# Moving the lower half of x to TensorE, converting two weight slices instead of four ahead of group 1, and taking scores ahead of y, in the ramp of a retention-plus-MLP kernel

## The chip, the cores and the metric

The kernel runs on one core of a Trainium2 chip. The metric is device time in microseconds (us) of one execution. Medians are quoted with the lowest and highest run.

## The reference

```python
def retnet(q, k, v):                 # each (4, 8, 768, 64): batch, head, position, dim
    for t in range(768):
        state = gamma[head] * state + outer(k[t], v[t])
        y[t]  = q[t] @ state / sqrt(64)

x = y.transpose(0, 2, 1, 3).reshape(3072, 512)
h = x @ w_in                         # w_in (512, 2048)
g = h * sigmoid(h)
out = g @ w_out                      # w_out (2048, 512)
```

The result must be close to float32, and the weights arrive as 64-bit floats, which the kernel puts together from their 32-bit words.

## The kernel before

The attention is computed in chunks of 128 positions. A *unit* is one chunk of one of 4 batches; the 24 units run through a pipeline of three stages, and a *visit* `m` does one stage of each of three units. Each float32 operand of the MLP becomes three fp32r parts (high, low, and a mixed term), so a *product* of a group `c` of 512 positions with a *slice* `f` of 128 columns of w_in is 12 matmuls: 8 into bank `ha`, 4 into `hb`. A slice costs eight VectorE instructions and three on ScalarE (`take_w`).

```python
def visit(m):
    first, mid, last = (0 <= m - i < len(units) for i in range(3))
    if first:
        stage_t(m)                       # transposes of k and q
    if last:
        scores, states_with, yp = stage_y(m - 2)
        scores()                         # y, first part
    if mid:
        sc, sums = score_tile(m - 1)
        stage_s(m - 1, sums)             # k^T v of both halves
    if last:
        states_with(0)                   # y, second part
    if mid:
        stage_a(m - 1, sc)               # scores
        ...
        finish_a(m - 1, sc, sums)        # VectorE: mask am, state
        scale_q(m - 1)                   # VectorE; at a new chunk GpSimd first scales gq
    ...
    if last:
        states_with(1)                   # y, third part
        finish_y(m - 2, yp)              # copy y, split it into x's three parts
```

The parts of y add into one pair of banks of PSUM, in which the kernel places TensorE's results. Between two parts stands a fence: GpSimd writes a one-element `token` when the last matmul of one part is done, and the next part waits for the token. GpSimd also makes the decay `gq` of the next chunk:

```python
def fence(done, then):
    i = nc.gpsimd.memset(token, 0.0).ins     # after done, ahead of then

def next_chunk():
    nc.gpsimd.tensor_tensor(out=gq, in0=gq, in1=step..., op=mult)
```

The order of TensorE's instructions is as written. On the other engines a list scheduler fixes an order of the instructions when the program is built. The trace of the kernel before fits that: ScalarE was idle for 3.27 us up to 33.66 us, where a step of a weight slice came, though y's last matmul had ended at 31.18 us; the copy of y ran at 35.58, behind two steps of that slice. The ramp:

```python
first = {6: (0, 0), 7: (0, 1), 8: (0, 2), 9: (0, 3)}
for m in range(10):
    if m in (0, 2, 4, 6):
        take_w()                         # four slices in the ramp
    visit(m)
    if m in first:
        product_in(*first[m])            # one product behind each of visits 6 to 9
...
pairs = [(1, f) for f in range(4)]       # then (1, f), each followed by visit 10 + f
```

## Time and profile before

| | before |
|---|---|
| median of the runs beside the change | 659.8 us (658.86 to 661.53) |
| profiled span | 658.1 us |
| TensorE busy | 619.1 us |
| TensorE idle | 39 us |

The prediction below shows where the idle time lies. In the views of the profile PE is TensorE (PEld its weight loads), DVE VectorE, ACT ScalarE and POOL GpSimd. A line gives start and length in us, engine, line of the kernel, operation, what it writes and reads, and in brackets the idle time before it and what ended it; "issue" means that the profile names nothing. Two more views are needed later. First, busy time by stretch. The columns are the stretch, its length, then busy us and count of PE, PEld, DVE, ACT and POOL, then the granted clock, the DMA share and GB/s:

```profile
20.00:45.00 25.00, 17.73 (x504) 15.71 (x501) 22.54 (x42) 12.76 (x25) 1.94 (x9) 0.80 0.87 197
45.00:80.00 35.00, 31.52 (x657) 25.87 (x659) 30.04 (x54) 21.35 (x37) 1.75 (x9) 1.00 0.73 182
80.00:140.00 60.00, 56.26 (x578) 46.10 (x569) 53.62 (x97) 37.20 (x66) 1.51 (x7) 0.97 0.64 186
```

VectorE (the third pair) is busy for 22.54 of 25 us in the first stretch. Second, GpSimd in order of time. It has next to nothing to do (14.5 us in all), so nothing in the page points to it:

```profile
36.69 1.04 POOL L280 TENSOR_TENSOR gq<-gq,step 128x512 f32<-128x512 f32 x1 [6.01 <-DVE qt L324]
37.67 0.09 POOL L307 MEMSET token<- 1x1 f32 x1
```

Already here the token runs right behind the decay multiplication, which had waited for VectorE (`qt`). TensorE was itself held until about 36 us, by a late copy of y, so it cost little.

### The profile page before, as it was taken

What the parts mean: (1) busy time and instruction counts of PE and PEld (TensorE: products, weight loads), DVE (VectorE), ACT (ScalarE), POOL (GpSimd) and SP (SyncE); (2) the same over time, 40 slices, a digit from 0 to 9 for tenths busy, and PEclk for the clock granted to TensorE, in tenths of its full rate; (3) what the DMA queues carried; (4) which work ended last, traced back from release to release, by engine and by line L of the source; (5) the groups of instructions that cost most, each with busy time, mean ns of one, the idle gap of its engine ahead of it and who ended that gap; (6) DMA issues with size and microseconds to landing.
All of it is one profiled execution on the core that took longest, in us unless ns stands there. A gap on an engine that the chain in (4) does not pass through costs nothing.

```text
span 658.1 us, 13540 instructions
## 1 busy us (share of the span) xinstructions
PE 619.1 (94%) x5440; PEld 509.5 (77%) x5440; DVE 429.4 (65%) x736; ACT 287.7 (44%) x522; POOL 14.5 (2%) x94
## 2 busy tenths in 40 slices
PE   4779989899999899999989999999999999999996
PEld 3667778788877777888768888888888888888885
DVE  3898899876968867667958856555463645554631
ACT  4556556655645344445437873222131412222311
POOL 3000000000000000000000000000000000000000
PEclk9879999999999899999999999999999999999999
DMA  9978685553477865757746744342342432433301
GB/s 202 215 163 209 169 213 167 167 185 128 172 260 171 215 179 162 225 176 218 242 135 202 205 162 151 97 161 96 97 159 97 136 121 96 160 90 103 128 0 65
DMA packets 123071, 103.65 MB, mean 157 GB/s; under 512 B 80000, under 2 KB 88192, under 8 KB 123008
## 3 DMA queue, kind: packets, MB, share of 16 engines
q1 hardware_dynamic: 119552, 96.49, 50.8%
q10 hardware_dynamic: 3456, 6.29, 2.6%
q8 instruction: 43, 0.70, 0.5%
q14 instruction: 20, 0.16, 0.1%
HBM read 66.06 MB, written 36.70 MB: 156 GB/s over the span
## 4 chain that ended last, share of the span: by engine, by line
PE 68%; DVE 17%; ACT 6%; DMA 5%; issue 3%; SPq 1%; ACTq 0%; DVEq 0%; POOLq 0%; POOL 0%
PE ha L489 15%; PE hb L489 8%; PE ob L620 7%; PE oa L618 7%; PE o L618 7%; PE o L620 7%; PE o L619 7%; PE oa L619 7%; DVE cs L200 2%; DVE cp L204 2%; DVE g L494 2%; DMA wf<-in_moe_w_in_dram 2%; PE y L391 2%; ACT g L495 1%; DMA wf<-in_moe_w_out_dram 1%
## 5 line engine op out<-in xcount | busy, mean ns | idle before, releaser
L489 PE MATMUL ha<-xt,wi 128*128 128x512 f32 x768 | 196.2, 397 | 6.4 <-DVE g L494 3.9
L489 PEld LDWEIGHTS ha<-xt,wi 128*128 128x128 f32 x768 | 142.8, 189 | 41.4 <-DVE g L494 7.3
L540 DVE TENSOR_TENSOR gs<-gr,gs 128x512 fp32r<-128x512 f32 x96 | 62.2, 686 | 90.3 <-ACT gs L538 90.3
L538 ACT ACTIVATE gs<-gr 128x512 fp32r<-128x512 f32 x96 | 53.5, 621 | 134.2 <-issue 131.8
L489 PE MATMUL hb<-xt,wi 128*128 128x512 f32 x384 | 103.4, 391 | 3.0 <-ACT g L493 2.8
L494 DVE TENSOR_TENSOR g<-g,hb 128x512 f32<-128x512 f32 x96 | 65.6, 684 | 45.2 <-PE hb L489 35.1
L495 ACT ACTIVATE g<-g 128x512 f32<-128x512 f32 x96 | 60.6, 631 | 76.0 <-DVE g L494 75.4
L489 PEld LDWEIGHTS hb<-xt,wi 128*128 128x128 f32 x384 | 71.8, 188 | 19.9 <-ACT g L493 3.9
L620 PE MATMUL ob<-wo,gs 128*128 128x512 f32 x192 | 75.2, 392 | 0.0
L618 PE MATMUL o<-wo,gs 128*128 128x512 f32 x192 | 74.7, 389 | 0.0
L620 PE MATMUL o<-wo,gs 128*128 128x512 f32 x192 | 74.7, 389 | 0.0
L618 PE MATMUL oa<-wo,gs 128*128 128x512 f32 x192 | 74.7, 389 | 0.0
L619 PE MATMUL o<-wo,gs 128*128 128x512 f32 x192 | 74.7, 389 | 0.0
L619 PE MATMUL oa<-wo,gs 128*128 128x512 f32 x192 | 74.7, 389 | 0.0
L493 ACT ACTIVATE g<-ha 128x512 f32<-128x512 f32 x96 | 56.5, 588 | 24.6 <-PE ha L489 20.1
L541 DVE SCALAR_TENSOR_TENSOR gs<-gs 128x512 fp32r<-128x512 f32 x96 | 62.0, 685 | 0.0
L620 PEld LDWEIGHTS ob<-wo,gs 128*128 128x128 f32 x192 | 36.0, 188 | 8.9 <-DVE o L626 1.6
L620 PEld LDWEIGHTS o<-wo,gs 128*128 128x128 f32 x192 | 36.0, 188 | 7.6
L619 PEld LDWEIGHTS o<-wo,gs 128*128 128x128 f32 x192 | 36.0, 188 | 7.5
L618 PEld LDWEIGHTS oa<-wo,gs 128*128 128x128 f32 x192 | 36.0, 188 | 7.5
L619 PEld LDWEIGHTS oa<-wo,gs 128*128 128x128 f32 x192 | 36.0, 188 | 7.5
L618 PEld LDWEIGHTS o<-wo,gs 128*128 128x128 f32 x192 | 36.0, 188 | 7.3
(80 smaller groups left out, 652.4 us busy)
## 6 DMA issues: line engine op xcount, KB each, us to landing
gd<-g SPq DMA_DIRECT2D x96, 256.0 KB, 2.9
gr<-gd SPq DMA_DIRECT2D x96, 256.0 KB, 2.7
wf<-in_moe_w_out_dram SPq DMA_DIRECT2D x16, 512.0 KB, 4.1
out_dram<-o ACTq DMA_DIRECT2D x24, 256.0 KB, 2.1
wf<-in_moe_w_in_dram SPq DMA_DIRECT2D x16, 256.0 KB, 3.3
wf<-in_moe_w_in_dram SPq DMA_DIRECT2D x32, 128.0 KB, 3.6
kf<-in_k_dram SPq DMA_DIRECT2D x16, 256.0 KB, 5.2
qf<-in_q_dram SPq DMA_DIRECT2D x16, 256.0 KB, 4.7
```

What stands on the lines that cost most here:

```text
L200: nc.vector.scalar_tensor_tensor(out=s, in0=a, scalar=3, in1=s, op0=ALU.logical_shift_left, op1=ALU.bitwise_or)
L204: nc.vector.scalar_tensor_tensor(out=p.bitcast(FP32), in0=lo, scalar=2.0 ** -52, in1=p.bitcast(FP32), op0=ALU.mult, op1=ALU.mult)
L489: nc.tensor.matmul(hb if i == 2 else ha, lhsT=w_sb[f][:, i, ts(kk, 128)], rhs=xt[c][:, i, kk, :], start=kk == 0 and i != 1, stop=kk == KIN ...
L493: nc.scalar.activation(out=hs, in_=ha, func=AF.Copy, scale=ONE_E)
L494: taken_out[:] = [nc.vector.tensor_tensor(out=hs, in0=hs, in1=hb, op=ALU.subtract).ins]
L495: nc.scalar.activation(out=hs, in_=hs, func=AF.Silu)
L538: nc.scalar.activation(out=t[:, 0, :], in_=g, func=AF.Copy, scale=HALF)
L540: nc.vector.tensor_tensor(out=t[:, 1, :], in0=g, in1=high, op=ALU.subtract)
L541: nc.vector.scalar_tensor_tensor(out=t[:, 2, :], in0=t[:, 1, :].bitcast(FP32), scalar=-1.0 / EPS, in1=high, op0=ALU.mult, op1=ALU.add)
L618: nc.tensor.matmul(oa, lhsT=gh, rhs=wo[f][:, 0, :], start=first_, stop=False)
L619: nc.tensor.matmul(oa, lhsT=glo, rhs=wo[f][:, 1, :], start=False, stop=last)
L620: nc.tensor.matmul(ob, lhsT=gm, rhs=wo[f][:, 2, :], start=first_, stop=last)
```

## The change

Three parts, with one intent: fewer VectorE instructions and a shorter way before the first product. The diff, cut:

```diff
@@ loads: one slice after units 2, 4 and 6
-        if n == 1:
-            load_w(1)
-        if n in (3, 5):
-            load_w(n // 2 + 1)
+        if n in (2, 4, 6):
+            load_w(n // 2)
@@ part 1: the lower half of x by TensorE, in y's own banks
+    minus = const.tile([128, 128], FP32R, ...)       # minus the identity
 def finish_y(n, yp):
+        if n < EARLY:                                # the first 8 units
+            nc.scalar.activation(out=xh, in_=yp, func=AF.Copy, scale=HALF)
+            lower[n] = yp, xh
+            return
+    def lower_x(n):
+        for o in range(2):
+            nc.tensor.matmul(yp[:, o], lhsT=minus, rhs=xh[:, o], start=False, stop=True, ...)
+        nc.scalar.copy(out=xl, in_=yp)
+        nc.vector.scalar_tensor_tensor(out=x[2], ...)
@@ part 3: scores ahead of y, in visits 0 to 9
+        lower_x(m - 3)
+        ramp = m < EARLY + 2
-        if last:
+        if last and not ramp:
             scores, states_with, yp = stage_y(m - 2)
             scores()
...
-            with tc.issue_after(taken_out[0]) if taken_out else ExitStack():
+            with tc.issue_after(taken_out[0]) if taken_out and not ramp else ExitStack():
                 finish_a(m - 1, sc, sums)
             scale_q(m - 1)
+        if last and ramp:
+            scores, states_with, yp = stage_y(m - 2)
+            scores()
+            states_with(0)
@@ part 2: two slices ahead of group 1's x
-    first = {6: (0, 0), 7: (0, 1), 8: (0, 2), 9: (0, 3)}
+    first = {6: (0, 0), 9: (0, 1)}
-        if m in (0, 2, 4, 6):
+        if m in (0, 4, 8):
             take_w()
...
-    pairs = [(1, f) for f in range(4)]
+    pairs = [(1, 0), (1, 1)] + [(c, f) for f in range(2, 6) for c in range(2)]
-    takes = [(1, 0), (1, 2)] + [(0, f) for f in range(4, half)]
-    takes += [(2, half), (2, half + 1)]
+    takes = [(1, 0)] + [(0, f) for f in range(2, half)]
+    takes += [(2, half - 4), (2, half - 2)]
```

In the ramp's first part, that leaves one product between visits 6 and 9 where there were three, and in group 1 a slice for each visit where there was one for every second. Part 3 also lifts, in the ramp, a rule that held `finish_a` (the mask and the state) behind the last product's `g`.

More of the change, by code (lines that the diff above doesn't have):

```diff
@@ L229 @@
             load(name, n)
-        if n == 1:
-            load_w(1)
-        if n in (3, 5):
-            load_w(n // 2 + 1)
+        if n in (2, 4, 6):
+            load_w(n // 2)
     ident = const.tile([128, 128], FP32, tag="ident", name="ident")
     make_identity(nc, ident)
+    minus = const.tile([128, 128], FP32R, tag="minus", name="minus")
+    nc.gpsimd.tensor_scalar(out=minus, in0=ident, scalar1=-1.0, scalar2=None, op0=ALU.mult)
     lag = const.tile([128, C], FP32, tag="lag", name="lag")
@@ L282, in next_chunk @@
                                 op=ALU.mult)
-    xt, kt, qt, am = {}, {}, {}, {}
+    xt, kt, qt, am, lower = {}, {}, {}, {}, {}
     taken_out = []
@@ L421, in finish_y @@
         raw = None
-        if c <= LATE:
+        if n < EARLY:
+            xh = xt[c][:, 0, :, ts(b, C)].rearrange("p a (o t) -> p o a t", o=2)
+            nc.scalar.activation(out=xh, in_=yp, func=AF.Copy, scale=HALF)
+            lower[n] = yp, xh
+            return
+        if c == LATE:
             raw = hpool.tile([128, KIN, C], FP32, tag="hs", name=f"ys_{n}")
             nc.scalar.copy(out=raw.rearrange("p a (o t) -> p o a t", o=2), in_=yp)
-            if c == LATE:
-                nc.sync.dma_start(out=y_dram[b], in_=raw)
+            nc.sync.dma_start(out=y_dram[b], in_=raw)
         split_x(c, b, yp, raw)
+    def lower_x(n):
+        if n not in lower:
+            return
+        c, b = units[n]
+        yp, xh = lower.pop(n)
+        x = [xt[c][:, i, :, ts(b, C)] for i in range(3)]
+        for o in range(2):
+            nc.tensor.matmul(yp[:, o], lhsT=minus, rhs=xh[:, o], start=False, stop=True,
+                             skip_group_check=True)
+        xl = x[1].rearrange("p a (o t) -> p o a t", o=2)
+        nc.scalar.copy(out=xl, in_=yp)
+        nc.vector.scalar_tensor_tensor(out=x[2], in0=x[1].bitcast(FP32), scalar=-1.0 / EPS,
+                                       in1=x[0].bitcast(FP32), op0=ALU.mult, op1=ALU.add)
     def split_x(c, b, y, raw):
@@ L462, in visit @@
             stage_s(m - 1, sums)
-        if last:
+        if last and not ramp:
             states_with(0)
@@ L558 @@
             put_g(1)
+    lower_x(EARLY - 1)
     half = NF // 2
-    pairs = [(1, f) for f in range(4)]
-    three = [x for f in range(4, half) for x in ((0, f), (1, f), (2, f - 4))]
-    rest = ([(2, f) for f in range(half - 4, NF - 4)] +
+    pairs = [(1, 0), (1, 1)] + [(c, f) for f in range(2, 6) for c in range(2)]
+    three = [x for f in range(6, half) for x in ((0, f), (1, f), (2, f - 6))]
+    rest = ([(2, f) for f in range(half - 6, NF - 4)] +
             [(c, f) for c in range(2) for f in range(half, NF - 4)])
@@ L567 @@
     steps = pairs + three + rest + last + groups
-    takes = [(1, 0), (1, 2)] + [(0, f) for f in range(4, half)]
-    takes += [(2, half), (2, half + 1)]
+    takes = [(1, 0)] + [(0, f) for f in range(2, half)]
+    takes += [(2, half - 4), (2, half - 2)]
     takes += [(0, half), (0, half + 2), (1, half), (1, half + 2)]
     takes += [x for x in (last + groups)[::3]][:NF]
-    behind = {(1, f): lambda f=f: visit(EARLY + 2 + f) for f in range(4)}
+    behind = {(1, 2 + i): lambda i=i: visit(EARLY + 2 + i) for i in range(4)}
     at = ([(1, NF - 1)] + [(2, f) for f in range(NF - 4, NF - 1)] +
```

## The prediction

> **What bounds the kernel now.** I read the page first (busy shares and the 40 slices), then the groups of the first 130 us, then TensorE, VectorE and ScalarE in order of time.
>
> ```profile
> PE 619.1 (94%) x5440; PEld 509.5 (77%) x5440; DVE 429.4 (65%) x736; ACT 287.7 (44%) x522; POOL 14.5 (2%) x94
> ```
>
> TensorE is busy for 619.1 of 658.1 us, so 39 us of idle time is nearly all there is to win. Nothing in the change shortens its work. Where the idle time lies comes from the busy times by stretch (columns: us, then busy us and count of PE, PEld, DVE, ACT, POOL, then granted clock, DMA share, GB/s):
>
> ```profile
> 20.70:27.90 7.20, 4.04 (x116) 3.56 (x116) 5.57 (x11) 4.07 (x8) 0.18 (x2) 0.77 0.90 203
> 27.90:37.10 9.20, 5.20 (x161) 4.68 (x164) 8.47 (x17) 5.03 (x11) 0.58 (x3) 0.87 1.01 224
> 37.10:44.00 6.90, 6.80 (x229) 6.15 (x221) 6.87 (x13) 3.66 (x7) 1.18 (x5) 0.67 0.72 180
> 69.90:98.00 28.10, 25.86 (x593) 21.60 (x593) 24.02 (x43) 16.05 (x29) 1.69 (x9) 0.97 0.75 194
> 98.00:130.00 32.00, 30.33 (x129) 24.44 (x128) 28.66 (x53) 20.33 (x36) 0.00 (x0) 0.97 0.54 164
> 400.00:500.00 100.00, 100.00 (x441) 82.35 (x440) 50.56 (x83) 24.46 (x45) 0.00 (x0) 1.00 0.37 119
> ```
>
> After 400 us TensorE is never free. Before 44 us it is idle for a third of the time while VectorE is nearly full. TensorE's gaps there, in order of time (the bracket is idle time and what ended it):
>
> ```profile
> 24.14 0.85 PE L391 MATMUL y<-am,kqv 64*64 64x64 f32 x32 [2.84 <-DVE am L367]
> 36.20 1.13 PE L391 MATMUL y<-am,kqv 64*64 64x64 f32 x32 [4.00 <-ACT ys L425]
> 43.98 2.12 PE L489 MATMUL ha<-xt,wi 128*128 128x512 f32 x8
> 68.91 2.48 PE L489 MATMUL ha<-xt,wi 128*128 128x512 f32 x8 [1.00 <-ACT xt L436]
> 95.92 0.27 PE L391 MATMUL y<-qt,mid 64*64 64x64 f32 x2 [1.86 <-issue]
> 128.98 1.20 PE L489 MATMUL hb<-xt,wi 128*128 128x512 f32 x4 [1.67 <-ACT g L493]
> ```
>
> The first product of the second half starts at 43.98 us. The two long gaps before it have one cause: in VectorE's fixed order a slice of weights stands ahead of the mask `am`, or ScalarE's share of that slice ahead of the copy of y. VectorE ahead of the second gap:
>
> ```profile
> 32.93 0.69 DVE L207 TENSOR_TENSOR cs<-cs,cp 128x512 f32<-128x512 f32 x1
> 34.32 0.69 DVE L119 SCALAR_TENSOR_TENSOR wil<-cs,wi 128x512 f32<-128x512 f32 x1 [0.69 <-ACT wi L117]
> 34.93 0.68 DVE L367 TENSOR_TENSOR am<-sc,decay 128x512 f32<-128x512 f32 x1
> ```
>
> So the early bound is VectorE, with the loads close behind: the transpose of k of unit 6 ran at 39.67 us, though its data came at about 36 us (issued at 30.79, median landing 5 us).
>
> [...] the 32 matmuls of y take 0.69 us warm, but 1.13 us after the 4.00 us gap, and the granted clock is 0.67 in the stretch that follows. [...] Here the high part of x took 0.63 us from SBUF and 0.60 us from PSUM (a later group, at 202.94 us), so the direct read saves almost nothing per instruction.
>
> **The change part by part.** A *unit* is one group of 128 positions of one batch, a *visit* a step of the three-stage pipeline over units. Visits 0 to 9 are the ramp.
>
> 1. *Lower half by TensorE.* Removed for 8 units: one VectorE subtraction (0.69 us; consecutive ones start about 0.60 us apart): 8 x 0.60 = 4.8 us of VectorE. Added: 16 matmuls of 256 columns. A product of 12 matmuls of 512 columns takes 2.72 us here, 0.227 each, so these are about 0.11 each, estimated 0.35 us per unit with the fill. ScalarE keeps its count: the copy `ys` goes (0.58), the copy of the lower half comes. But y's only pair of banks is now held until that copy: y ends, xh 0.63, matmul, copy 0.57.
>
> 2. *Two slices instead of four.* A slice costs VectorE 2 x 0.42 + 0.43 + 5 x 0.69 = 4.7 us, about 4.3 when other work fills its waits. Before, slices 0 to 3 were all asked for before visit 7; now 0 and 1 by visit 4, slice 2 at visit 8, slice 3 after the ramp. So some 8 us of VectorE work leave the stretch up to the first product. They are not saved: group 1's pairs now contain slices 4 to 7. The order of the built program confirms that slice 2's chain now stands beside `am` of unit 6, slice 3's beside `am` of unit 8.
>
> 3. *Scores ahead of y.* The mask gets its scores sooner after the transposes. It has a price: y's three parts follow one another, with a GpSimd fence between each two, where other matmuls used to stand in between. The late visits of the kernel before, which have nothing in between, show it:
>
> ```profile
> 339.44 0.69 PE L391 MATMUL y<-am,vf 64*64 64x64 f32 x32
> 340.44 0.27 PE L391 MATMUL y<-qt,state 64*64 64x64 f32 x2 [0.30 <-POOL token L307]
> 341.20 0.27 PE L391 MATMUL y<-qt,mid 64*64 64x64 f32 x2 [0.30 <-POOL token L307]
> ```
>
> From 339.44 to the end of y at about 341.65 us: 2.2 us, against 1.2 inside an interleaved visit. So 8 x 1.0 = 8 us of TensorE time spent, though mostly where it would otherwise wait.
>
> *A visit in the new ramp:* transposes 0.95, lower half 0.35, sums and scores 1.0, y 2.2: 4.5 us warm, say 4.6 with waits. Loads: from the first k at 6.83 to the second at 10.33 three tensors came, so 1.2 us each; a unit takes 3.5 us and a slice of weights 2.4. With slices after units 2, 4 and 6 that is 4.7 us per visit over the pairs, so TensorE and DMA are almost equal. VectorE needs 2.5 us per visit of chunk 0 and 3.1 of chunk 1, plus slices: no longer the bound before 40 us.
>
> *The schedule.* Visit 1 is set by loads and decays as before (scores of unit 0 end near 15.9). Visit 2, partly cold, ends near 21.5; visits 3 to 6 at 4.6 each end at 40. The product (group 0, slice 0) then starts at 40 instead of 43.98 and ends at 42.7. Visits 7 to 9: 13.8, plus about 1.0 because VectorE has slices 2 and 3 there (17 us of VectorE work for 14.8): 57.5. The second product ends at 60.2. With the last lower half and three more products this is 10 visits and 5 products at about 68.7. The kernel before has that at 72.5: 4 us won.
>
> Next, 4 visits and 14 products up to the 19th product. TensorE needs 4 x 3.1 + 14 x 2.72 = 50.5 us. The kernel before took from 72.5 to 130.2, 57.7: 7 us lost to the gaps above (1.86 and 1.67), a product that ran cold at 96.19 (3.69 instead of 2.11), and small waits. After the change a pair with a visit needs 2 x 2.72 + 3.1 = 8.5 us of TensorE and of VectorE 4.3 + 2 x 0.6 + 3.7 = 9.2, over three to four of them: some 3 us of new stalls, partly absorbed by a lead of two slices. So 54 us, at 122.7, and a gain of 7.5 to 9 by then. After that both kernels run the same steps; the waits of about 10 us between 195 and 334 us stay.
>
> Sum: 660.2 - 8.5 = 651.7; I put 651.5.
>
> **Rivals.** (a) *VectorE stays the bound*: the two slices come back in group 1's pairs. For it: VectorE is already busy for 24.0 of 28.1 us in that stretch, and each slice has a round trip to ScalarE. Against: 4.8 us are really saved. Then the gain is the 4.8 us or less: 655 to 658. (b) *The chain through y's banks and fences sets the visits*: if xh, matmul and copy do not fit beside transposes and scores, a visit costs over 5.2 us, five visits lose 3 us before the first product and the ramp gains nothing: 656 to 660. For it: one pair of banks and ScalarE strictly in order. Against: ScalarE has only 2.4 us per visit of chunk 0. (c) *TensorE never stops*: warm through the ramp, no stall later, as the early lead takes out the order of transfers behind the 1.67 us gap. Then 12 to 15 us go: 645 to 648.
>
> **Range and chances.** Between (a) and (c) lies 645.5 to 657. Faster by over 2% needs under 647.0, a gain of 13.2 us, a third of all idle time: 0.14. Within 2%: 0.84. Slower by over 2% has no mechanism here that costs 13 us: 0.02.
>
> **What would show it.** The first `ha` near 40 us; the gaps of 2.84 and 4.00 us gone; y with fences of 0.3 us in the ramp; 8 fewer VectorE instructions and 16 more matmuls; five products and ten visits by 69 us; TensorE gaps after VectorE between 70 and 100 us of 3 us in sum. I am wrong if the first product comes before 37 or after 43 us, if TensorE waits over 5 us on VectorE in group 1's pairs, or if the time after 130 us changes.

That TensorE can make y - xh in y's banks was an assumption when it was written. "Warm" in it means a granted clock near 1 (the 32 matmuls of y took 0.69 us at 28.96, with 1.00 granted between 28.96 and 31.10 us), "cold" a lower one (1.13 us at 36.20, with 0.50 granted between 36.20 and 41.50 us). Its 0.35 us for the correction is an estimate from 0.227 us a matmul; its "fill" was not measured. In the change the two matmuls took 0.48 us warm, and the next began 0.41 us after their start (41.28 and 41.69 us). For "ScalarE strictly in order" the traces show the case given above, 3.27 us idle up to 33.66 us.

## The result, and the profile after

The change made the kernel slower: 666.6 us (666.07 to 668.1, 4 runs) against 659.8 us. The ratio is 1.0104, with a 95% interval of 1.0076 to 1.0131. Ratios here are the mean time of one kernel's fast runs over the mean of the other's fast runs of the same rounds, so not quite the ratio of the quoted medians. The prediction said 651.5 and at most 657.

```profile
PE 619.2 (93%) x5456; PEld 509.6 (77%) x5456; DVE 424.1 (64%) x728; ACT 288.8 (43%) x522; POOL 15.7 (2%) x95
```

The counts are as foretold: 16 more matmuls, 8 fewer VectorE instructions. TensorE is busy for the same 619 us, so the whole loss is idle time: 664.3 - 619.2 = 45 us against 39. By stretch, with the columns of before:

```profile
20.00:45.00 25.00, 17.74 (x524) 15.31 (x521) 17.40 (x33) 11.40 (x22) 2.17 (x11) 0.93 0.92 206
45.00:80.00 35.00, 28.82 (x485) 23.96 (x484) 26.75 (x49) 20.01 (x34) 1.99 (x7) 0.95 0.53 138
80.00:140.00 60.00, 53.73 (x718) 43.89 (x717) 52.04 (x94) 36.15 (x64) 1.75 (x9) 1.00 0.66 185
```

The first row shows the intent fulfilled: VectorE fell from 22.54 to 17.40 us there. TensorE did not gain from it; it is busy for 17.74 us where it was 17.73. In the next two rows it loses 2.7 and 2.5 us. TensorE's gaps name the places:

```profile
29.31 0.69 PE L350 MATMUL sc<-kqv 64*64 64x64 f32 x32 [1.84 <-issue]
33.15 0.45 PE L392 MATMUL y<-qt,mid 64*64 64x64 f32 x8 [2.21 <-POOL token L308]
36.22 1.13 PE L350 MATMUL sc<-kqv 64*64 64x64 f32 x32
44.94 2.11 PE L515 MATMUL ha<-xt,wi 128*128 128x512 f32 x8
52.05 0.69 PE L392 MATMUL y<-am,kqv 64*64 64x64 f32 x32 [1.87 <-ACT xt L446]
60.76 0.27 PE L392 MATMUL y<-qt,mid 64*64 64x64 f32 x2 [2.65 <-POOL token L308]
91.58 0.66 PE L334 MATMUL kp<-ident,kf 128*128 128x128 f32 x4 [1.33 <-DVE g L520]
102.20 0.66 PE L334 MATMUL kp<-ident,kf 128*128 128x128 f32 x4 [1.40 <-DVE g L520]
113.54 0.66 PE L334 MATMUL kp<-ident,kf 128*128 128x128 f32 x4 [1.59 <-DVE g L520]
123.77 2.14 PE L515 MATMUL ha<-xt,wi 128*128 128x512 f32 x8 [1.31 <-DVE g L520]
```

Four kinds of wait. For the 1.84 us the profile names nothing; VectorE's addition to the `state`, which frees the bank of `sc`, ended at 29.21 us behind the last steps of a slice, so I take it to be the cause (in e9 the profile names it, 1.93 us). The gaps of 2.21 and 2.65 us are for GpSimd's token, and GpSimd shows why:

```profile
32.03 1.04 POOL L281 TENSOR_TENSOR gq<-gq,step 128x512 f32<-128x512 f32 x1 [6.32 <-DVE qt L325]
33.01 0.09 POOL L308 MEMSET token<- 1x1 f32 x1
```

The token needs 0.09 us. In GpSimd's built order it stands behind the multiplication of the next chunk's decay, and that waits 6.32 us for VectorE to be done with the old decay (`qt`). In the program the multiplication belongs to visit 5 (`scale_q` of the first unit of chunk 1). In the built kernel before it stands behind the two fences of visit 4, in the built changed kernel ahead of them: the scheduler moved it, once y stood last in the visit. The second one, at 59.26 us, likewise went ahead of a fence of visit 8.

The 1.87 us gap is y's banks, held for the copy of the lower half. ScalarE ahead of it:

```profile
49.11 1.28 ACT L521 ACT_TABLE_LOAD   x1
50.41 0.63 ACT L521 ACTIVATE g<-g 128x512 f32<-128x512 f32 x1
50.94 0.57 ACT L336 COPY qt<-qp 128x512 f32<-128x512 f32 x1
51.41 0.59 ACT L446 CAST xt<-y 128x512 fp32r<-128x512 f32 x1
```

The copy at 51.41 stands behind the first Silu (h * sigmoid(h) of the reference), whose function table is loaded just before. The kernel before loads the same table at 50.38 us, but there the copy that frees y's banks is not behind a correction by TensorE.

The 1.3 to 1.6 us gaps in group 1 wait for `g`, the subtraction that frees `hb`'s bank for the next transposes (for the next product at 123.77 us). VectorE was busy for 9.33 of the 10.62 us between 91.58 and 102.20 us, a slice being in it.

"Done" in this table is the start of what follows.

| milestone, us | predicted | before | after |
|---|---|---|---|
| end of visit 3 | 26.1 | 27.93 | 26.14 |
| first product starts | 40 | 43.98 | 44.94 |
| visits 7 to 9, length | 14.8 | between products | 19.2 |
| 10 visits and 5 products done | 68.7 | 72.5 | 78.63 |
| 14 visits and 19 products done | 122.7 | 130.01 | 137.54 |

### The profile page after: what moved, and what is told of

It is laid out like the page before. It is cut to its first block, busy times and chain, and to the rows that moved or that the text cites. A ratio compares the mean times of both kernels' runs of the same rounds, so it can differ in the third digit from the quotient of the medians.

```text
span 664.3 us, 13549 instructions
## 1 busy us (share of the span) xinstructions
PE 619.2 (93%) x5456; PEld 509.6 (77%) x5456; DVE 424.1 (64%) x728; ACT 288.8 (43%) x522; POOL 15.7 (2%) x95
## 4 chain that ended last, share of the span: by engine, by line
PE 71%; DVE 15%; ACT 5%; DMA 4%; issue 3%; SPq 1%; POOL 1%; ACTq 0%; POOLq 0%; DVEq 0%
PE ha L515 17%; PE hb L515 9%; PE ob L647 7%; PE o L646 7%; PE oa L646 7%; PE o L647 7%; PE o L645 7%; PE oa L645 7%; PE y L392 2%; DVE g L520 2%; DMA wf<-in_moe_w_in_dram 2%; DVE cp L204 2%; DVE cs L200 2%; DVE ca L197 1%; DMA wod<-cw 1%
## 5 line engine op out<-in xcount | busy, mean ns | idle before, releaser
L515 PE MATMUL ha<-xt,wi 128*128 128x512 f32 x768 | 193.9, 394 | 6.5 <-DVE g L520 5.0
```

Of the source, the lines that this page charges most:

```text
L515: nc.tensor.matmul(hb if i == 2 else ha, lhsT=w_sb[f][:, i, ts(kk, 128)], rhs=xt[c][:, i, kk, :], start=kk == 0 and i != 1, stop=kk == KIN ...
```

## The experiments

Four names for the theories. **FENCE**: GpSimd's multiplication ahead of the token. **BANK**: y's banks are held too long by TensorE's correction. **VECTOR** (in some expectations SLICES or DENSITY): slices on VectorE stop TensorE wherever they stand. **FILLER**: visits need a product between them, to cover the round through the other engines. The kernel before is the yardstick of each ratio; by itself it ran between 656.46 and 663.26 us in the first batch, and up to 665.11 in a later one, so a ratio within 0.4% of another says little.

| run | what | median, us | ratio to before, 95% |
|---|---|---|---|
| after | parts 1, 2, 3 | 666.60 | 1.0104 (1.0076 to 1.0131) |
| e7_only_lower | part 1 | 667.22 | 1.0084 (1.0030 to 1.0138) |
| e4_only_slices | part 2 | 661.91 | 1.0021 (0.9975 to 1.0067) |
| e5_only_order | part 3 | 663.45 | 1.0042 (0.9993 to 1.0091) |
| e2_old_visits | parts 1, 2 | 669.70 | 1.0136 (1.0087 to 1.0185) |
| e3_four_slices | parts 1, 3 | 672.97 | 1.0193 (1.0150 to 1.0237) |
| e9_slices_order | parts 2, 3 | 669.72 | 1.0131 (1.0082 to 1.0181) |
| e1_fence_first | after, fence first | 664.81 | 1.0059 (1.0002 to 1.0116) |
| e6_fence_silu | e1, table early | 664.82 | 1.0071 (1.0028 to 1.0113) |
| e17_fill_eight | e6, product moved | 660.56 | 1.0028 (0.9989 to 1.0066) |
| e8_three_slices | e6, three slices | 660.48 | 1.0008 (0.9966 to 1.0050) |
| e16_three_only | after, three slices | 668.05 | 1.0128 (1.0107 to 1.0148) |
| e12_three_single | e8, thinner tail | 661.78 | 1.0019 (0.9982 to 1.0057) |
| e10_slices_fence | e4, fence first | 662.46 | 1.0022 (0.9979 to 1.0066) |
| e13_before_three | before, three slices and both repairs | 657.59 | 0.9959 (0.9920 to 0.9998) |
| e14_spread_takes | e13, slices spread | 657.04 | 0.9968 (0.9930 to 1.0007) |
| e19_spread_again | e14 again | 658.41 | 0.9993 (0.9962 to 1.0024) |
| e15_before_pool_act | before, both repairs | 659.27 | 0.9999 (0.9966 to 1.0032) |
| e18_two_single | e14, two slices | 659.86 | 1.0010 (0.9975 to 1.0045) |

One caution on these times. From the 19th product on all kernels do nearly the same work, yet that rest took 526.5 to 531.1 us in the traces, at mean granted clocks of 0.99 to 1.00. So a lead of 2 or 3 us at the 19th product can vanish in the time of a run, and each milestone below is that of a single trace.

All gave correct results; so did the change, so TensorE can add into y's banks after ScalarE has read them, as its 16 added matmuls do. For the prediction that was still an assumption.

### The first batch: mend the fence, and undo one part at a time

**e1_fence_first**, the change with the multiplication issued only behind the last fence so far:

```diff
+    tokens = []
 def fence(done, then):
...
+    tokens[:] = [i]
 def next_chunk():
-    nc.gpsimd.tensor_tensor(out=gq, ...)
+    with tc.issue_after(tokens[0]):
+        nc.gpsimd.tensor_tensor(out=gq, ...)
```

> The changed kernel, with one order on GpSimd altered: the multiplication that makes the next chunk's table gq may be issued only after the last fence of y issued before it, so that it no longer stands ahead of the fences of units 2 and 6. Nothing else is edited. Theory FENCE (the ramp lost its gain because GpSimd, in order, held y's fence behind gq, which waits for VectorE; waits of 2.21 and 2.65 us, each followed by a cold stretch of TensorE in visits 5 and 9): both waits fall to 0.3 us, 1.9 + 2.35 us go at once and some 2.9 us of cold matmuls with them, so about 7 us faster than the changed kernel: 659.5 us (657 to 662), the first product at 41 to 42 us. Rival VECTOR (VectorE sets the pace of the ramp, and the waits only move): at most 3 us faster, 663 us or more. Rival BANK (y's only pair of banks and the chain through it sets the visits): also 663 or more, with the waits for the copy of the lower half growing.

```profile
42.08 2.14 PE L519 MATMUL ha<-xt,wi 128*128 128x512 f32 x8
49.21 0.69 PE L396 MATMUL y<-am,kqv 64*64 64x64 f32 x32 [1.87 <-ACT xt L450]
```

The first product came at 42.08 instead of 44.94, and the granted clock between 20 and 45 us was 1.00 instead of 0.93: FENCE holds for the first 2.9 us of this trace: visit 4 became 1.9 us shorter, and visit 5, which now ran at full clock, 1.1 us. Not all of that is sure to be the repair: e6 and e17, with the same repair and the same order up to there, start the first product at 43.51 and 41.92 us, e6 with a clock of 0.93 again. The time, 664.81, lies where VECTOR and BANK had put it (663 or more) and not in FENCE's 657 to 662, and its interval overlaps that of the change. The 1.87 us wait stayed, and visit 9 now took 7.9 us, with a stop of 2.35 us that is told under e6. The lead over the change was 3.7 us at the 19th product (133.88 against 137.54); the rest took 529.9 us against 526.8, though with the same 3565 matmuls: they kept TensorE busy for 515.2 us against 511.7, at a granted clock of 0.99 against 1.00.

**e2_old_visits**, the change without part 3:

```diff
-        ramp = m < EARLY + 2
+        ramp = False
```

> The changed kernel with the third part undone: the visits of the ramp have the old interleaved order, lower half ahead of y. The built order has gq behind the fences again, as the kernel before has. FENCE: the waits of 2.2 and 2.65 us on the token go, but y's scores now follow directly on the matmul of the lower half and wait for ScalarE's copy, an estimated 1.2 us in each of 8 visits, against 1.0 us per visit saved at the fences: 659 to 663 us. BANK: those waits are longer, 1.5 to 2.5 us each, and the run is no faster than the changed kernel, 666 to 672. VECTOR: no change, 665 to 668.

The estimate of 1.2 us is as much as the 0.63 us of `xh` and the 0.57 us of a copy in the prediction.

```profile
51.05 0.70 PE L392 MATMUL y<-am,kqv 64*64 64x64 f32 x32 [2.96 <-ACT xt L446]
```

This is one of eight waits for the lower-half copy, seven ahead of y and one ahead of a product, 10.6 us in sum: in the old order y comes right behind the transposes, and its banks are not free then. The token waits are gone, and still the run is no faster: BANK's range (666 to 672) holds, FENCE's (659 to 663) does not. With part 3, in the change, one such wait of over 0.45 us is left, 1.87 us. That part 3 helps part 1 does not show in the times: the intervals of e2 and the change overlap, and parts 1 and 3 together (e3, 1.0193) are slower than part 1 alone (e7, 1.0084).

**e3_four_slices**, the change without part 2:

```diff
-    first = {6: (0, 0), 9: (0, 1)}
+    first = {6: (0, 0), 7: (0, 1), 8: (0, 2), 9: (0, 3)}
-        if m in (0, 4, 8):
+        if m in (0, 2, 4, 6):
...                                  # loads, pairs and takes as before
```

> The changed kernel with the second part undone: four slices asked for in the ramp, their loads and the order of products as in the kernel before; lower half by TensorE and the new order of visits stay. gq stands ahead of a fence here too by the built order. FENCE: not cured, and as VectorE reaches the scaling of q later behind more slices, the wait on the token is as long or longer: 664 to 671. VECTOR or a theory SLICES (the two slices put into group 1's pairs cost what they save): TensorE's waits on VectorE there (6.2 us in the changed kernel between 85 and 125 us) mostly go, 657 to 661.

The first product started at 51.15 us, behind waits of 3.65 us for ScalarE's upper half of x and 3.05 us for a token. With VectorE full the multiplication ahead of the token waits longer still. The time is above FENCE's range (664 to 671) and far above that of SLICES (657 to 661).

**e4_only_slices**, the kernel before with part 2 alone (the last hunk of the diff and the loads):

> The kernel before with the second part alone: two slices ahead, the new order of loads and of products; lower half by VectorE, old order of visits. FENCE (the second part is sound): VectorE is relieved by two slices before the first product, its waits of 2.84 and 4.00 us shrink, first product at 39 to 41 us; group 1's pairs lose 4 to 6 us more than before: 656 to 661. SLICES (the second part is the culprit): 664 to 668.

The first product started at 39.19 us, so two slices do what they were for. The lead was gone by the end of group 1's pairs (19 products at 131.25 us, against 130.01 before): four waits for `g` of 1.17 to 1.53 us there, 5.3 us in sum, and a stop of 1.35 us in the midst of a group of matmuls. The time lies between the two ranges.

### The second batch: the other combinations, and the next repair

**e5_only_order**, the kernel before with the part 3 hunk alone:

> The kernel before with the third part alone: in the first ten visits TensorE takes the scores first and all of y after them; four slices are still converted ahead of group 1's x and VectorE still makes the lower half. BANK says that the new order is worth something only to shorten the time for which y's one pair of banks is held; here the banks are freed by one copy as before, so the time is that of the kernel before within 0.3%, 658.5 to 662.5. CHAIN (the order itself is bad, because all of y now stands behind the scores and the three-pass chain of each visit gets longer) says 663 to 666, with first-product start at 45 or later instead of 43.98. VECTOR (four slices keep VectorE behind, so a longer distance between scores and y helps) says 655 to 658.

BANK's expectation missed, and CHAIN, a rival named only here, met both of its marks: 663 to 666 us, and a first product at 45 us or later (48.25). The largest wait was again a token's, 3.76 us at 36.20, behind the multiplication; the next, 2.99 us, was for the `state`. So part 3 alone brings the trap, but how much of the delay is the trap and how much the order itself is not shown: part 3 with the fence mended, without the other parts, was not run. The ratio's interval includes 1, so in time it is not settled.

**e9_slices_order**, the change without part 1: `finish_y` as before, no `lower_x`.

> Parts two and three without the first: two slices ahead, scores ahead of y, the lower half by VectorE as before. If the loss of the change is the price of the first part (y's banks held across TensorE's correction), this run stands at that of part two alone or better, 658 to 662, and TensorE has no wait of 1.8 us on the upper half or the lower copy before y's first product. If the loss is the price of order and missing products behind visits 7 and 8 (FILLER), it stands within 2 us of the changed kernel, 664 to 668, with visits 7 to 9 at 6 us each although nothing waits for TensorE's correction.

This was the greatest surprise for the theory that part 1 is to blame: without it the kernel was no faster than with it. The trace has token waits of 2.48 us at 33.80 and 2.85 us at 60.81, the same two as in the change, so FENCE has a part in it, 5.3 us of waits. But FILLER had nearly foreseen it: no faster than the change, 664 to 668 us (it was 669.72), and visits 7 to 9 of some 6 us each with no correction to wait for (they took 19.8 us in sum). This run does not tell the two apart; with the fence mended it was not run.

**e6_fence_silu**, e1 with the Silu table loaded early:

```diff
             first_chunk()
+            nc.scalar.activation(out=token2, in_=token2, func=AF.Silu)
```

> The changed kernel with the decay multiplication held behind the last fence (as in e1) and ScalarE's Silu table loaded early by a dummy activation. SILU says: the table load of 1.28 us stood ahead of the lower-half copy that frees y's banks and made most of the 1.87 us wait near 49 us; without it that wait falls below 0.8 us and the time is 1.2 to 1.9 us under e1, 662.9 to 663.6. Rival: the copy stands behind Silu and q's copies anyway, the wait stays above 1.4 us, and the time is that of e1 (664.8) within 0.7.

The wait fell from 1.87 to 0.46 us and visit 7 from 6.5 to 5.1 us, as SILU said, but the time did not move (664.82, where the rival had put it). Visit 9, up to the product behind it, now took 8.6 us. VectorE and TensorE in it:

```profile
58.25 0.42 DVE L195 TENSOR_SCALAR cs<-wf 128x512 uint32<-128x512 uint32 x1
58.59 0.41 DVE L386 TENSOR_TENSOR state<-mid,sc 128x256 f32<-128x256 f32 x1
```

```profile
59.10 0.69 PE L356 MATMUL sc<-vf,kf 64*64 64x64 f32 x32 [1.19 <-issue]
63.61 0.27 PE L398 MATMUL y<-qt,mid 64*64 64x64 f32 x1 [2.12 <-issue]
```

The first wait names nobody, but the bank of `sc` is free only when VectorE has added the `state`, which ended at 59.0 us behind an instruction of the next slice; I infer the cause from that order. The second is of another kind: TensorE stopped in the midst of a part of y, all of whose matmuls wait for one token. Nothing in the trace releases it. e1 has the same stop (2.35 us at 63.37), and the 1.86 us gap of the kernel before at 95.92 also lies within a part of y. The last section gives those of the kernel before and of the change.

**e8_three_slices**, e6 with a third slice and a product behind visit 7:

```diff
-    first = {6: (0, 0), 9: (0, 1)}
+    first = {6: (0, 0), 7: (0, 1), 9: (0, 2)}
-        if m in (0, 4, 8):
+        if m in (0, 3, 6):
-    pairs = [(1, 0), (1, 1)] + [(c, f) for f in range(2, 6) for c in range(2)]
+    pairs = [(1, 0), (1, 1), (1, 2)] + [(c, f) for f in range(3, 6) for c in range(2)]
...                                  # takes to match
```

> e6 with three slices ahead of group 1's x instead of two, and a product behind each of visits 6, 7 and 9. FILLER says that visits 7 and 8 of the changed kernel took some 6.4 us instead of 4.5 because no product stood between them to hide the chain of one visit on ScalarE, VectorE and GpSimd; a product behind visit 7 then costs less than its 2.7 us in the ramp, ten visits and five products end at most 1 us later than in e6 minus nothing for the product moved, and the time is 658 to 661.5. SLICES says that VectorE's added 5.6 us of a third slice ahead of group 1's x holds the visits up by as much, and the time is 663 to 668, above e6.

The 5.6 us for a slice is the author's estimate, without a source; the prediction counted 4.7.

```profile
47.09 0.60 PE L340 MATMUL kp<-ident,kqv 128*128 128x128 f32 x4
52.05 2.11 PE L522 MATMUL ha<-xt,wi 128*128 128x512 f32 x8
54.92 0.60 PE L340 MATMUL kp<-ident,kf 128*128 128x128 f32 x4
59.88 0.66 PE L340 MATMUL kp<-ident,kf 128*128 128x128 f32 x4
64.49 2.11 PE L522 MATMUL ha<-xt,wi 128*128 128x512 f32 x8
```

Visit 7 starts at 47.09 and ends where the product starts, at 52.05; visit 8 runs from 54.92 to 59.88, visit 9 from there to 64.49: 5.0 + 5.0 + 4.6 = 14.5 us; the prediction gave those three 14.8, though with no product between them. In e6 they took 18.4, and 3.3 of the 3.9 us between are the two waits of its visit 9, of which e8 has none. Each of its four runs was under each of e6's in the same batch, and the interval against before includes 1. So the three parts of the change can be carried without a loss that these runs can see (up to 0.5% is not excluded), but not with a gain.

### The third batch: part 1 alone, and the thinner tail

**e7_only_lower**, the kernel before with part 1 alone:

> The kernel before with the first part alone: four slices ahead, the old order of the visits, the lower half of x by TensorE in y's banks. It has the products behind visits 6 to 9 and so loses no filler. If the correction in y's banks has a price of its own (BANK), TensorE waits before y's first product for the lower-half copy or before the correction for the upper half in most visits, 6 us or more in sum, and the time is 666 to 672. If the price was only that of missing products (FILLER alone), it stays within 0.4% of the kernel before, 657.5 to 663, or below it, for VectorE has eight instructions less.

```profile
42.38 0.69 PE L394 MATMUL y<-am,kqv 64*64 64x64 f32 x32 [2.27 <-ACT xt L448]
53.05 0.77 PE L394 MATMUL y<-am,kqv 64*64 64x64 f32 x32 [2.96 <-ACT xt L448]
```

BANK is shown, and FILLER does not apply, since products stand behind visits 6 to 9. Seven such waits ahead of y and one ahead of a product sum to 12.8 us, though each part also replaces waits that the kernel before has. Part 1 alone costs 0.8%.

**e10_slices_fence**, e4 with the fence repair of e1:

> Part two alone (as in e4) with GpSimd's decay multiplication held behind the fence ahead of it. FENCE says: in e4 the multiplication stood ahead of a fence near 59 us and cost TensorE 2.4 us there, and a smaller wait near 33 us; with it behind, the token waits of over 0.5 us go and the time falls by 1.5 to 2.5 us, 659.4 to 660.4. Rival (VECTOR): VectorE's q scaling that the multiplication waits for is as late as before, what waited at the fence waits at the next scores, and the time is that of e4, 661.5 to 662.5.

FENCE missed; the time is where VECTOR had put it (661.5 to 662.5). In the old order one of the visit's two fences is issued after `scale_q`, so the repair left the multiplication between the two, and a token wait of 1.72 us remained at 59.63 (2.39 in e4). There the multiplication did not wait for VectorE: it took 3.27 us itself (3.29 in e4), where it takes 1.04 in most places. The waits for `g` in the pairs were there as in e4, 4.5 us in sum.

**e12_three_single**, e8 with group 1's tail as before:

```diff
-    pairs = [(1, 0), (1, 1), (1, 2)] + [(c, f) for f in range(3, 6) for c in range(2)]
+    pairs = [(1, 0), (1, 1), (1, 2), (0, 3), (1, 3)]
-    takes = [(1, 0), (1, 1)] + [(0, f) for f in range(3, half)]
+    takes = [(1, 0), (1, 2)] + [(0, f) for f in range(3, half)]
...                                  # steps and visits after these as before
```

> e8 (all three parts, three slices ahead, products behind visits 6, 7 and 9) with the tail of the ramp as the kernel before has it: one product behind each of visits 10 to 12 and two ahead of visit 13, and a slice only at every second of them. DENSITY says: with a slice in every pair VectorE had 9.1 us of work in 10.2 to 10.6 us of each pair and TensorE lost 1.3 us at each visit (4.7 us in e8); with half the slices there it loses 0 to 1.5 us, and the time is 656.5 to 658.5, under the kernel before. Rival: the slices that are not converted there are short afterwards, TensorE stops for a w slice or for g in the products that follow, and the time is 659.5 to 662 as in e8.

DENSITY missed, and its rival (659.5 to 662) holds. The four waits for `g` of e8 in the pairs (1.37, 1.40, 0.59 and 1.00 us) became one of 2.37 us and a stop in the midst of a group of 1.42 us, but the 19th product ended no earlier than in e8 (133.7 against 132.8 us).

**e13_before_three**, the kernel before with three slices, both repairs and e12's tail; no part 1, no part 3:

> The kernel before with three slices ahead instead of four, products behind visits 6, 7 and 9, the multiplication behind the fence, the Silu table loaded early, and the tail as in e12: no correction by TensorE, and the old order of the visits. If TensorE's correction with the new order has no worth of its own once there is a product to fill the visits, this stands at or under e12, 654 to 658. If VectorE's eight instructions less pay, it stands over e12 by 1 to 3 us, 658 to 661.

It has 14 visits and 19 products done at 126.6 us, against 130.0 before, and its ratio was just under 1. So TensorE's correction and the new order together have no worth of their own here; e13 drops both, and does not tell one from the other. A wait of 1.89 us for `g` at 188.95, which the kernel before lacks, took back part of the lead.

### The fourth and fifth batch: what was still open

**e17_fill_eight**, e6 with one product moved:

```diff
-    first = {6: (0, 0), 9: (0, 1)}
+    first = {6: (0, 0), 8: (0, 1)}
```

> e6 (two slices, all three parts, the fence and the Silu table mended) with nothing changed but the place of one product: the second product of group 0 stands behind visit 8 instead of visit 9. FILLER (visits 7 to 9 of the changed kernel are long because no product stands between them, so that the round through ScalarE, VectorE and GpSimd is exposed): the three visits and the product take 2 us less than in e6, where visit 7 starts at 46.4 and visit 10's work at 80.1; the time falls to 662 to 663.3. VECTOR (visit 9 is long because the third slice's nine VectorE instructions stand ahead of the state's addition there, wherever the product is): the stop moves but the sum stays, the time is that of e6 within 0.8 us, 664 to 665.6.

The time was under what FILLER expected, but the intervals of e17 and e6 overlap, the batches differ, and the profiled run of e17 was its slowest (665.18). In that trace visit 9 took 6.0 us instead of 8.6 (the slice has eight VectorE instructions, not the nine of the expectation): the 1.19 us wait for the `state` was gone, and so was most of the unexplained stop. The product behind visit 9, which now ran in another place, was slow (3.37 instead of 2.11 us for its first eight matmuls). From the start of visit 7 to that of visit 10 the trace took 33.0 us, against 33.7 in e6, where FILLER had said 2 us less. So the times speak for FILLER and this trace does not; neither is shown.

**e16_three_only**, e8 without the two repairs:

> The changed kernel with three slices ahead and products behind visits 6, 7 and 9, as e8, but with the decay multiplication ahead of the fence and the Silu table loaded late, as in the change. e8 was 5.8 us faster than the changed kernel by ratio; e1 and e6 alone, which hold the multiplication behind the fence, were 2 to 3 us faster. If the two gains add, this run is 3 us slower than e8: 663 to 664.5, with a token wait of over 2 us near 33 us. If the third slice and its product hide the fence as well, it is within 1 us of e8, 660 to 661.5.

This is the clearest pair: 1.0128 without the repairs, 1.0008 with them, intervals far apart. The waits are back: 1.63 us for a token at 32.63, 1.87 us for the lower-half copy at 51.80, 1.78 us for a token at 62.10. Without the repairs the third slice was worth nothing, so the two gains do not add; each needs the other. The gain lies in visits 7 to 9: 19.9 us here and 14.5 in e8, while the first product comes at 44.69 here and at 44.22 there.

**e15_before_pool_act**, the kernel before with both repairs alone:

> The kernel before with only the multiplication behind the fence and the Silu table loaded early; four slices, the order and the products as before. e13 (657.6, ratio 0.9959) has these two and three slices instead of four. If the third slice count is what wins, this run equals the kernel before within 0.2%, 659.5 to 662. If the two small repairs win, it stands where e13 does, 657 to 659.

The repairs are worth nothing to the kernel before: its multiplications are not ahead of a fence that TensorE would otherwise pass, and no correction waits behind its table load.

**e14_spread_takes**, e13 with two slices spread:

```diff
-    takes += [(2, half), (2, half + 1)]
+    takes += [(2, half - 4), (2, half - 2)]
```

> e13 with slices 10 and 11 converted after the products (2, 4) and (2, 6) instead of (2, 8) and (2, 9). In e13 TensorE stood 1.89 us at 188.95 us for VectorE's g, a wait that the kernel before does not have, and lost there most of a lead of 3.6 us over the kernel before at 19 products. If two slices in a row on VectorE made that wait, it falls below 0.5 us and the time is 655 to 656.6, ratio 0.993 or under. Rival: the wait comes from the loads or from a later slice and stays; the time is that of e13, 656.8 to 658.5.

The wait at 189 us went, as expected; the time did not follow beyond the spread of the runs, and 657.04 is in the rival's range (656.8 to 658.5).

**e19_spread_again**, the same kernel in five rounds:

> The kernel of e14 unchanged, in five rounds, to settle whether it is under the kernel before: e14 gave 0.9968 with an interval that just includes 1. If it is, the ratio is 0.995 to 0.998 with an upper end under 1.

It missed: 0.9993, with 1 inside the interval. What looked like 0.3 to 0.4% in e13 and e14 is not established (e13 itself was not run again).

**e18_two_single**, e14 with two slices instead of three:

```diff
-    first = {6: (0, 0), 7: (0, 1), 9: (0, 2)}
+    first = {6: (0, 0), 9: (0, 1)}
-        if m in (0, 3, 6):
+        if m in (0, 4, 8):
...                                  # pairs to match
```

> e14 with two slices ahead instead of three: part two of the change in the old order, without TensorE's correction, with both repairs, and one slice in every second visit of group 1 instead of one in each. If the dense pairs are what part two loses by (e10, with a slice in every pair, was at ratio 1.0022 and lost 4.5 us to VectorE's g in the pairs), this gains 2 to 3 us on e10, ratio 0.995 to 0.999, at or above e14. If two slices are too few whatever comes after, because visits without a product stand behind VectorE's third slice, the ratio stays at 1.001 to 1.004.

1.0010 is the lower end of the second expectation, and its interval covers both, so it tells nothing apart. No run shows a version that is really faster than the kernel before.

## Why the prediction was wrong

**The direction and the size.** It said 8.5 us faster; it was 6.8 us slower by the medians, and the time is 15.1 us off. Two of its own three signs of being wrong came true: a first product after 43 us, and over 5 us of waits for VectorE in group 1's pairs. The milestones split the error into three nearly equal shares: 4.9 us up to the first product (44.94 against 40), 5.0 us from there to five products (33.7 against 28.7), 4.9 us in group 1 (58.9 against 54).

**What held.** The counts of instructions; VectorE's relief before 45 us; visits 2 and 3, which ended at 21.6 and 26.1 us as reckoned (21.5 and 26.1); a sound visit, 4.50 us from 40.44 to 44.94 against "4.5 us warm, say 4.6"; the fences' own price of 0.3 us each in a sound visit. The gaps of 2.84 and 4.00 us went. So the arithmetic of instructions was right, and the error lies in what they wait for.

**The step that failed first: "visits 3 to 6 at 4.6 each end at 40".** Visit 4 took 8.1 us and visit 5 6.2. Visit 4 has the 2.21 us token wait, and the 1.84 us that I put down to VectorE's state addition behind a slice; visit 5 ran in part at a lower clock (0.72 granted between 34.25 and 40.44 us). The prediction priced a fence from the late visits, where nothing stands ahead of the token on GpSimd, and took 0.3 us as its price everywhere. It compared the built orders for VectorE's slices only; GpSimd's would have shown four tokens ahead of the first multiplication instead of six. With the repair the first product came 2.9 (e1), 1.4 (e6) and 3.0 us (e17) earlier, and e9 and e5 showed that part 3 brings the trap without part 1. The 1.84 us stayed in all three, and no run tests its cause; with three slices ahead the repairs brought the first product forward by 0.5 us only (e8 against e16).

**Second: "Visits 7 to 9: 13.8, plus about 1.0".** They took 19.2 us: visit 7 6.5 us with the table load ahead of the copy, visit 8 6.9 us with the second multiplication ahead of a token, visit 9 5.9 us with part of it at a lower clock (0.71 granted between 61.15 and 67.05 us). Four runs share the rest of the change and show what it takes:

| visits 7 to 9, us | no repair | both repairs |
|---|---|---|
| two slices, no product between | 19.2 (the change) | 18.4 (e6) |
| three slices, a product behind visit 7 | 19.9 (e16) | 14.5 (e8) |

So the predicted length was reached, but only with both. Without the repairs y's banks, freed only by ScalarE's copy, and the tokens tie TensorE to what stands ahead of them in ScalarE's and GpSimd's order. Without the product between, the repaired visits stop elsewhere, 1.19 us for the `state` and 2.12 us within a part of y (e6). The prediction's own bracket, 17 us of VectorE work for 14.8, does not fit its added 1.0 us either, if all of that work was due there; in the change VectorE was busy for 15.3 of the 19.2 us.

**Third: "some 3 us of new stalls" in the pairs.** The mechanism was right and its size wrong. The reckoned 9.2 us of VectorE work in a pair was 9.3 in the pair measured above, but that pair lasted 10.6 us: VectorE also waited, 1.15 us of it for ScalarE's first step of the next slice, which stands behind the copies of the next visit's transposes. The four waits for `g` summed to 5.6 us where 3 were reckoned, and "partly absorbed by a lead of two slices" did not happen. e4 shows the same waits with part 2 alone.

**"After that both kernels run the same steps"** held nearly: 526.8 us against 528.1 from the last milestone to the end.

**The rivals.** (b), the chain through y's banks and fences, was the right neighbourhood, and the waits in e7 and e2 show its bank half. It was given 656 to 660, for it only cancelled the gain; no rival let the change cost time. The chance of 0.84 for within 2% covered the outcome, the range did not.

**What stays open.** Why TensorE stops for 1 to 2 us in the midst of a group of matmuls; how the gain of e8 over e6 divides between the third slice's place and the product behind visit 7; and what part 3 costs by its order alone, without the trap.

## What to carry to other kernels

Before an order is changed, read what stands ahead of each short signal on the engine that sends it, even if that engine is 2% busy: a 0.09 us token behind a multiplication that waits for a third engine held TensorE for 2.2 and 2.7 us. When a PSUM bank is freed by a second engine's later copy instead of its first, price that copy by its place in that engine's order, with a table load where one is due. And price a wait from the stretch where it will stand, not from a later one where its engine is free.

## What the traces show of the clock, the table load and the stops

- After the 2.21 us gap of the change (up to 33.15) the matmuls from 36.22 to 38.00 us had a granted clock of 0.50: two groups took 1.13 and 1.08 us, against 0.69 and 0.65 in a sound visit. In the kernel before, groups of 0.85 and 1.13 us followed the gap of 2.84 us, of 1.13 and 1.08 us that of 4.00 us. The length of the gap alone does not tell: after a gap of 1.84 us (at 29.31) and one of 1.87 us (at 52.05) in the change the same kind of group took 0.69 us, while in the kernel before the product behind the gap of 1.86 us took 3.69 instead of 2.11 us, with 0.55 granted between 96.19 and 100.00 us. No rule for it is shown.
- The table load took 1.28 us. In the change the copy ahead of it ended at 49.10 us, the load began at 49.11, and the Silu at 50.41.
- TensorE stopped within a group of matmuls that all wait for the same token (1.86 us in the kernel before, 2.35 in e1, 2.12 in e6). Between 17 and 400 us the kernel before and the change have three stops of 0.45 us and more in the midst of a group for which the profile names nothing: 0.69 us at 58.48 and 1.86 us at 95.92 in the kernel before, 0.62 us at 105.65 in the change. Each ended 1.26 to 1.47 us after a 16 KB packet of the profile's DMA queue q8 had ended, but each of the two traces has 34 such packets in that time, most without a stop behind them. Whether the two belong together was not tested; what ends the stops is not shown.
